# Attention and SwiGLU on one core: first scores and packing behind M, last output products inside the next batch's first chunk

## Chip, core and metric

The kernel runs on one core of one Trainium2 chip. The metric is device time in microseconds (us), as the median of several runs; less is better. The engines are called PE (TensorE: matmuls), DVE (VectorE), ACT (ScalarE), POOL (GpSimd) and SP (SyncE, which here only issues DMAs).

## What is computed

Two steps of attention, then a gated feed-forward layer, all in float32:

```python
batch, n_heads, seq, head_dim = (8, 8, 576, 64)
n_pack = 32
n_tokens, d_model, d_ff = (4608, 512, 1536)

def sm_attn(qq, kk, vv):
    s = scale * np.matmul(qq, kk.transpose(0, 1, 3, 2))
    s = s - np.max(s, axis=-1, keepdims=True)
    a = np.exp(s)
    a = a / (np.sum(a, axis=-1, keepdims=True) + 1e-09)
    return np.matmul(a, vv)
p_packed = sm_attn(p, k, v)              # 32 rows for each head
out = sm_attn(q, p_packed, p_packed)     # 576 rows for each head
...
g = x @ w_gate                           # x: out, heads side by side
silu = g * (1.0 / (1.0 + np.exp(-g)))
val = x @ w_val
return (silu * val @ w_out).astype(np.float32)
```

## The kernel before

**Tiles.** x itself is never formed. For each batch the kernel multiplies the packed rows by the gate and value weights; this product is called M, comes in six pieces k (`m_mm`, tile `w` by `ppt`, 64-row tiles of 32 columns), and is split into a high and a low part (`mh` on ACT, `ml` on DVE). The second attention's weights, also split (`a2h`, `a2l`), times M give gate and value directly. Every large product is made of three matmuls (high by low, low by high, high by high).

**Loops.** A batch b runs through 12 chunks fc of the inner width. A chunk has an A half (256 token columns) and a B half (320). Each half (`gv_chunk`) is a gate product and a value product of six matmuls each, into the two PSUM banks of the pool `ps_gv`: the gate bank is read by ACT (Silu into `sg`), the value bank by DVE (`hf`, and in B halves the 64 columns in `t`, kept in `t4`). ACT then makes `hh` from `hf` and DVE makes `hl`. With two banks in the pool, the next half's gate product waits for `sg`, and its value product for `hf` and `t`. Behind each half PE does six output matmuls (`out_mm` into `acc`) of the chunk before. In chunks of odd number M's next piece follows the A half.

**Filling.** While batch b runs, the attention of batch d = b + 1 is worked in between: scores of the first attention (`q_scores`, two groups of 32 matmul records), their maxima and differences on DVE (`q_read`), exponentials on ACT (`q_exp`), sums and a trip of the sums through DRAM (`q_sums`, `q_gather`: one DMA out, four back into `x`), common factors (`q_common`, `q_common_exp`, `q_factors`), scaling and transposing (`q_turn`), the packing product (`q_pack`, 160 records of 32 columns) and its transpose into `ppt`; then the second attention in two halves (`s2_mm`, `s2_block`, `s2_max`, `s2_exp`, `s2_sums` and `s2_scale`, `s2_turn`, `s2_high`, `s2_low`). `plan_of` says at which place of which chunk each step is issued. A place is a count of pieces of PE work in the chunk (1, 2: behind A's gate and value; 3, 4: behind the two output products; 5, 6 and 7, 8: the same for B) or "a", "ha" ("b", "hb"): behind the Silu of A (of B), and between `hh` and `hl`.

**Order.** PE runs in the order in which the code is written. DVE, ACT and SP are ordered by a scheduler, except that what goes through `pin` keeps the order of the program. Batch 0 has a hand-written order of its own (`PROGRAM`), ending in the output products of its last halves (`out22`, `out23`).

**End of a batch.** Behind chunk 11 come the last 12 output matmuls, then `end` copies the four `acc` banks out (`emit_out`). Behind each odd batch, the 64-column remainders of two batches, collected in `t4`, go through 36 more output matmuls into one bank `p4`:

```python
            outs(NFC - 1, 0, lambda: None)
            outs(NFC - 1, 1, lambda: None)
            end(rows, accs)
            if b % 2:
                p4 = ps()
```

Of the kernel before, what the change touches and what calls it, by code (L numbers as in the profile page):

```python
# [54 lines left out]
    out21 Ml:6.2 hl22 s2_low1 g23 s2_back0 silu23 out22 h23 hh23 s2_high0 hl23 s2_low0 out23  # L55
# [4 lines left out]
def tile_pack_attention_swiglu(ctx: ExitStack, tc: tile.TileContext, qT, kT, v, vq, pT, wgv, wout, out):  # L60
# [338 lines left out]
    def q_pack(b, half):  # L399

        if half == 0:
            sq[b].append(ps())
        a1, p_p = sq[b][4:]
        v_t = vs[b]
        for hp in range(2 * half, 2 * half + 2):
            for k in range(NKQ):
                for g in range(P // NP):
                    par, ds = g // 2, slice(g % 2 * NP, g % 2 * NP + NP)
                    nc.tensor.matmul(  # L409
                        p_p[NP * g : NP * g + NP, NP * hp : NP * hp + NP],  # L410
                        a1[:, par, hp, k, :], v_t[:, par, hp, k, ds],
                        start=(k == 0), stop=(k == NKQ - 1),
                    )
        if half:
            ppts[b] = pool.tile([P, P], F32, tag="ppt", bufs=2, name="ppt")
            pin(nc.vector.transpose(ppts[b], p_p[:, :P]))
            del sq[b], vs[b]
# [115 lines left out]
    def h_split(src, hi, lo, between=lambda: False):  # L533
        hh = pool.tile([P, 256], F32R, tag="hh", bufs=3, name="hh")
        hl = pool.tile([P, 256], F32R, tag="hl", bufs=3, name="hl")
# [54 lines left out]

    def plan_of(b):

        d, plan = b + 1, {}

        def at(fc, place, *todo):
            plan.setdefault((fc, place), []).extend(todo)

        if d < B:
            c, c2 = (1, 0) if d % 2 else (0, 1)
            cs, cs2 = slice(c, c + 1), slice(c2, c2 + 1)
# [4 lines left out]
            at(1, "ha", lambda: q_scores(d, 1, gv_ps), lambda: q_read(d, 1, (0, 1)))  # L608
            at(1, 8, lambda: q_sums(d, 0))
            at(2, "a", lambda: q_exp(d, 1))  # L610
            at(2, 8, lambda: q_sums(d, 1), lambda: q_gather(d))
            at(3, 8, lambda: q_common(d))
            if d + 1 < B:
                at(3, 8, lambda: load_k(d + 1))
            at(4, "a", lambda: q_common_exp(d))
            at(4, 4, lambda: q_factors(d))
            at(4, 8, lambda: q_turn(d, 0))
            at(5, 8, lambda: q_turn(d, 1))
            at(6, 4, lambda: q_pack(d, 0))
            at(6, 8, lambda: q_pack(d, 1))  # L620
            if d + 1 < B:
                at(7, "ha", lambda: load_v(d + 1))
            at(7, "ha", lambda: s2_tiles(d), lambda: s2_a2(d))
            at(7, "ha", lambda: s2_mm(d, c, gv_ps), lambda: s2_block(d, c))
# [4 lines left out]
            at(9, "ha", lambda: s2_mm(d, c2, gv_ps), lambda: s2_block(d, c2))  # L629
            if d + 1 < B:  # L630
                at(9, "ha", lambda: load_q(d + 1))
            at(9, 4, lambda: s2_low(d, c))
            at(9, 8, lambda: s2_max(d, cs2))
            at(10, "a", lambda: s2_exp(d, cs2))
            at(10, 4, lambda: s2_sums(d, cs2), lambda: s2_scale(d, cs2))
            at(10, 8, lambda: s2_turn(d, c2), lambda: s2_high(d, c2))
            at(11, 4, lambda: s2_low(d, c2))
        return lambda fc, place: bool([f() for f in plan.pop((fc, place), ())])

    with tc.manual_schedule(engines={mybir.EngineType.PE}):  # L640
# [6 lines left out]
        def begin(b):  # L647
            odd = b % 2
            if not odd:
                t4[b // 2] = pool.tile([P, NFC, P], F32, tag="t4", bufs=1, name="t4")  # L650
# [4 lines left out]
        def end(rows, accs):  # L655
            for i, r in enumerate(rows):
                emit_out(accs[i], r, i % 2)


        with tc.manual_schedule(  # L660
# [61 lines left out]
            rows, accs = begin(0)  # L722
# [121 lines left out]
        end(rows, accs)  # L844

        steady[0] = True
        for b in range(1, B):
            rows, accs = begin(b)
            run = plan_of(b)
            ha, hb = {}, {}  # L850

            def outs(fc, which, fill):
# [5 lines left out]
            for fc in range(NFC):  # L858
                count = [0]

                def fill():
# [10 lines left out]
                    if count[0] in (4, 8):  # L872
# [11 lines left out]
            end(rows, accs)  # L884
            if b % 2:
                p4 = ps()
                t4_t = t4.pop(b // 2)
                for fc in range(0, NFC, 2):
# [42 lines left out]
```

## Time and profile before

| | us |
|---|---|
| median of 3 runs (747.27 to 747.54) | 747.53 |
| span of the profiled execution, first to last instruction | 745.3 |
| what lies around the span (747.53 - 745.3) | 2.2 |
| PE busy | 732.5 (98%) |
| DVE busy | 456.8 (61%) |
| ACT busy | 368.8 (49%) |
| mean granted TensorE clock | 1.000 |

In rows of the timeline the first number is the start in us from the start of the span and the second is the time from the first start to the last end of the instructions merged in the row ("x2" are two). Ends of matmuls are modelled, and one begins long before the end of the one ahead of it. So this document reads PE's pace from starts: a row of x2 that begins at 237.10 and is followed by one at 237.34 took 0.24 us, whatever its own length says. In the groups the numbers behind the bar are busy us, mean ns of one, and idle us before them with what ended most of it.

### The profile page before, as it was taken

To read this page: it belongs to the slowest core of one execution; us is meant where nothing else is said; L and a number is where in the kernel's file an instruction comes from. 1 tells how busy PE (TensorE), PEld (TensorE's weight loads), DVE (VectorE), ACT (ScalarE), POOL (GpSimd) and SP (SyncE) were. 2 spreads that over 40 slices of the span, in tenths; PEclk is the share of its full clock that TensorE was granted. 3 is DMA by queue.
4 is the path that set the end of the run, shared out by engine and by line. 5 is a ranking of instruction groups with operands and counts; after the bars stand their busy time and mean duration, and the time that the engine had idled before them with its cause. 6 is when DMAs were issued, how large, how long until landed. Compare 5 with 4: busy or idle time off the path is not lost.

```text
span 745.3 us, 15149 instructions
## 1 busy us (share of the span) xinstructions
PE 732.5 (98%) x6288; PEld 594.8 (80%) x6288; DVE 456.8 (61%) x1008; ACT 368.8 (49%) x666; POOL 2.0 (0%) x13
## 2 busy tenths in 40 slices
PE   7999999999999999999999999999999999999998
PEld 5756666888788887887888888888888888888886
DVE  5988878665755557645765556655575555744334
ACT  3777755754516445563544535464452644533331
POOL 0000000000000000000000000000000000000000
PEclk9999999999999999999999999999999999999999
DMA  9696483201112021302112011100201000010001
GB/s 350 255 326 254 175 323 113 69 3 73 64 71 69 2 73 64 124 4 71 66 57 83 3 72 64 58 3 1 72 2 72 3 1 2 1 57 1 1 1 72
DMA packets 20005, 59.16 MB, mean 79 GB/s; under 512 B 5984, under 2 KB 7008, under 8 KB 17376
## 3 DMA queue, kind: packets, MB, share of 16 engines
q1 hardware_dynamic: 19792, 58.12, 21.6%
q8 instruction: 50, 0.82, 0.5%
q14 instruction: 19, 0.16, 0.1%
q10 hardware_dynamic: 144, 0.07, 0.0%
HBM read 48.69 MB, written 9.49 MB: 78 GB/s over the span
## 4 chain that ended last, share of the span: by engine, by line
PE 90%; DVE 5%; ACT 2%; issue 1%; DVEq 0%; ACTq 0%
PE gv L557 34%; PE acc L576 30%; PE aux L194 7%; PE gv L745 6%; PE acc L786 4%; PE aux L576 4%; PE aux L409 1%; PE gv_aux L194 1%; ACT L456 1%; PE acc L645 1%; DVE r L463 1%; DVE s L452 1%; DVE hf L568 1%; DVE hl L538 1%; DVE r L451 1%
## 5 line engine op out<-in xcount | busy, mean ns | idle before, releaser
L564 ACT ACTIVATE sg<-gv 128x256 f32<-128x256 f32 (+1 forms) x168 | 68.9, 410 | 165.3 <-PE gv L557 138.6
L557 PE MATMUL gv<-a2h,ml 128*128 128x256 f32 (+1 forms) x672 | 147.0, 300 | 1.8 <-DVE t L571 1.1
L568 DVE TENSOR_TENSOR hf<-gv,sg 128x256 f32<-128x256 f32 x168 | 70.8, 421 | 121.3 <-PE gv L557 99.3
L557 PE MATMUL gv<-a2l,mh 128*128 128x256 f32 (+1 forms) x672 | 144.0, 296 | 0.0
L557 PE MATMUL gv<-a2h,mh 128*128 128x256 f32 (+1 forms) x672 | 143.9, 295 | 0.0
L576 PE MATMUL acc<-wo_h,hl 128*128 128x512 f32 x344 | 140.7, 409 | 1.4 <-DVE hl L778 1.4
L576 PE MATMUL acc<-wo_l,hh 128*128 128x512 f32 x344 | 135.6, 394 | 0.0
L576 PE MATMUL acc<-wo_h,hh 128*128 128x512 f32 x344 | 134.5, 391 | 0.0
L557 PEld LDWEIGHTS gv<-a2h,ml 128*128 128x128 f32 x672 | 115.0, 189 | 18.4 <-PE gv L557 4.1
L105 ACT CAST hh<-hf 128x256 fp32r<-128x256 f32 x168 | 67.8, 403 | 102.8 <-DVE hf L568 102.8
L538 DVE TENSOR_TENSOR hl<-hf,hh 128x256 fp32r<-128x256 f32 x168 | 70.5, 420 | 78.3 <-ACT hh L105 78.3
L557 PEld LDWEIGHTS gv<-a2h,mh 128*128 128x128 f32 x672 | 108.4, 190 | 0.0
L557 PEld LDWEIGHTS gv<-a2l,mh 128*128 128x128 f32 x672 | 108.2, 189 | 0.0
L576 PEld LDWEIGHTS acc<-wo_h,hl 128*128 128x128 f32 x344 | 64.7, 188 | 37.0 <-issue 26.4
L576 PEld LDWEIGHTS acc<-wo_h,hh 128*128 128x128 f32 x344 | 64.6, 188 | 14.9
L576 PEld LDWEIGHTS acc<-wo_l,hh 128*128 128x128 f32 x344 | 64.8, 188 | 8.3 <-issue 0.5
L497 DVE TENSOR_TENSOR ml<-aux,mh 128x512 fp32r<-128x512 f32 x92 | 59.0, 683 | 4.7 <-ACT mh L523 3.6
L194 PE MATMUL aux<-w,ppt 64*32 64x512 f32 (+1 forms) x784 | 52.4, 588 | 0.5 <-ACT mh L523 0.5
L523 ACT CAST mh<-aux 128x512 fp32r<-128x512 f32 x92 | 49.2, 586 | 4.9 <-PE aux L194 1.9
L564 ACT ACT_TABLE_LOAD x30 | 38.5, 1283 | 16.4 <-PE gv L557 16.1
L786 PE MATMUL acc<-wo_f,h 128*128 128x512 f32 x80 | 37.2, 595 | 0.0
L786 PEld LDWEIGHTS acc<-wo_f,h 128*128 128x128 f32 x80 | 14.3, 189 | 13.8 <-issue 13.2
(152 smaller groups left out, 753.9 us busy)
## 6 DMA issues: line engine op xcount, KB each, us to landing
st<-in_wgv SPq DMA_DIRECT2D x12, 1024.0 KB, 6.3
k_t<-in_kT SPq DMA_DIRECT2D x16, 576.0 KB, 4.9
q_t<-in_qT SPq DMA_DIRECT2D x16, 576.0 KB, 4.9
out<-ot SPq DMA_DIRECT2D x36, 256.0 KB, 2.1
v_t<-in_vq SPq DMA_DIRECT2D x6, 1280.0 KB, 5.7
st<-in_wout SPq DMA_DIRECT2D x6, 1024.0 KB, 5.5
v_t<-in_v SPq DMA_DIRECT2D x2, 1024.0 KB, 8.7
p_t<-in_pT SPq DMA_DIRECT2D x7, 64.0 KB, 2.5
```

What stands on the lines that cost most here:

```text
L105: e.copy(dst, src)
L194: nc.tensor.matmul(outs[par][32 * hp : 32 * hp + 32], lhs(r, hp), rhs(r, hp), start=True, stop=True)
L409: nc.tensor.matmul(p_p[NP * g : NP * g + NP, NP * hp : NP * hp + NP], a1[:, par, hp, k, :], v_t[:, par, hp, k, ds], start=(k == 0), stop=( ...
L497: pin(nc.vector.tensor_tensor(*lows.pop(0), op=ALU.subtract))
L523: nc.scalar.copy(m[0][at], src)
L538: low = lo.tensor_tensor(hl, src, hh.bitcast(F32), op=ALU.subtract)
L557: nc.tensor.matmul(pg[:, :n], m_[:, g, f, s * P : (s + 1) * P], a_[:, g, off : off + n], start=(i == 0), stop=(i == 5),)
L564: nc.scalar.activation(sg[:, :n], pgs[0][:, :n], AF.Silu)
L568: nc.vector.tensor_tensor(hf, pgs[1][:, o : o + 256], sg[:, o : o + 256], op=ALU.mult)
L576: nc.tensor.matmul(acc[:, :], h_[:, c : c + P], w_[fc // 2][:, fc % 2], start=(fc == 0 and i == 0), stop=(fc == NFC - 1 and i == 2),)
L745: nc.tensor.matmul(held[i][s][:, :n], m_[:, g, f, s * P : (s + 1) * P], a_[:, g, off : off + n], start=(j == 0), stop=(j == len(todo) - 1),)
L786: nc.tensor.matmul(accs[2 * is_b + c], half(i)[:, c * P : c * P + P], wos[fc // 2][:, fc % 2], start=(fc == 0), stop=(fc == NFC - 1),)
```

## The change

Three things change.

1. The plan becomes two tables of places, one for d = 2 (`FIRST`) and one for all later batches (`LATER`). In `LATER` the first group of scores moves from chunk 0 of batch b to chunk 11 of the batch before it (chunk number -1), straight behind M's piece there, and into the gate and value banks (`gv_ps`) in place of the `aux` banks. In both tables the whole packing product is one step (`pack`) behind M's piece of chunk 5, also in a gate or value bank, in place of two halves at the ends of A and B in chunk 6. Many steps on DVE and ACT get other places: sums, common factors and turns come earlier, `max0` is issued in front of the B half of chunk 7, `sums0` between `hh` and `hl` of chunk 8's A half, `turn_0` and `turn_1` between `hh` and `hl` of a B half.
2. The output products of a batch's chunk 11 are no longer done at its end but behind the A and B half of the next batch's chunk 0 (`behind`). For batch 0 `out22` and `out23` go the same way. Behind an odd batch the 12 output matmuls stay where they were, and the 36 of `p4` go behind these two halves, 24 and 12. The bank `p4` and the splitting of `t4` have tiles of their own (`hh4`, `hl4`, two each).
3. `fill` now calls the plan at every count.

```diff
-        if d < B:
...
-            at(0, 2, lambda: q_scores(d, 0))
-            at(0, "ha", lambda: q_read(d, 0, (0,)))
-            at(0, "hb", lambda: q_read(d, 0, (1,)))
-            at(1, "a", lambda: q_exp(d, 0))
...
-            at(2, 8, lambda: q_sums(d, 1), lambda: q_gather(d))
-            at(3, 8, lambda: q_common(d))
-            at(4, "a", lambda: q_common_exp(d))
...
-            at(6, 4, lambda: q_pack(d, 0))
-            at(6, 8, lambda: q_pack(d, 1))
...
-            at(7, 8, lambda: s2_max(d, cs))
-            at(8, "a", lambda: s2_exp(d, cs))
-            at(8, 4, lambda: s2_sums(d, cs), lambda: s2_scale(d, cs))
-            at(8, 8, lambda: s2_turn(d, c), lambda: s2_high(d, c))
...
+LATER = """
+    -1.ha q0 q0r q0s
+    -1.b q0e
...
+    2.4 q1z
+    3.ha common
+    3.5 common_e
...
+    5.ha pack
...
+    8.ha sums0
...
+        "q0": lambda d: q_scores(d, 0, gv_ps if d > 2 else ps),
+        "pack": lambda d: q_pack(d, gv_ps),
+        for d in (b + 1, b + 2):
...
+            for line in (FIRST if d == 2 else LATER).strip().splitlines():
...
+                fc = int(fc) + NFC * (d - b - 1)
+                if (0 if d > 2 else -NFC) <= fc < NFC:
...
-    def q_pack(b, half):
+    def q_pack(b, bank=ps):
-        for hp in range(2 * half, 2 * half + 2):
+        for hp in range(NHP):
...
+        def last_outs(rows, accs, out):
+            def last(which):
+                out(which)
+                for c in range(2 * which, 2 * which + 2):
+                    emit_out(accs[c], rows[c], c % 2)
...
                 if fc:
                     outs(fc - 1, 0, fill)
+                else:
+                    behind(0)
...
                 if fc:
                     outs(fc - 1, 1, fill)
-            outs(NFC - 1, 0, lambda: None)
-            outs(NFC - 1, 1, lambda: None)
-            end(rows, accs)
+                else:
+                    behind(1)
+                    for x, y in zip((rows, accs), accs_of(b)):
+                        x.extend(y)
+            last = last_outs(rows, accs, lambda which: outs(NFC - 1, which))
+            if not b % 2:
+                return last
...
+            def behind_p4(which):
+                if which == 0:
+                    p4.append(ps())
+                    for k in range(4):
+                        mm4(k)
+                        split4(k + 2)
+                else:
+                    mm4(4, 5)
+                    emit_out(p4[0], (b // 2) * 2 * S + 4 * P, 0)
+
+            t4_t = t4.pop(b // 2)
+            split4(0, 1)
+            for which in range(2):
+                last(which)
+            return behind_p4
```

How rows move, at three places. The first is PE from M's piece in chunk 11 of batch 2 (`w_81` by `ppt`) to chunk 0 of batch 3; `acc` rows are output matmuls, `gv` rows gate and value products, `k_t,p_t` scores. Of each run the first row is shown. Before:

```order
L194 MATMUL aux<-w_81,ppt 32x512 x8
L576 MATMUL acc<-wo_h,hl 128x512
...
L557 MATMUL gv<-a2h,ml 128x320 x2
...
L576 MATMUL acc<-wo_h,hl 128x512
...
L557 MATMUL gv<-a2h,ml 128x256 x2
...
L323 MATMUL aux<-k_t,p_t 32x144 x16
L557 MATMUL gv<-a2h,ml 128x320 x2
```

And in the changed kernel:

```order
L257 MATMUL aux<-w_81,ppt 32x512 x8
L386 MATMUL gv_aux<-k_t,p_t 32x144 x16
L635 MATMUL acc<-wo_h,hl 128x512
...
L616 MATMUL gv<-a2h,ml 128x320 x2
...
L635 MATMUL acc<-wo_h,hl 128x512
...
L616 MATMUL gv<-a2h,ml 128x256 x2
...
L635 MATMUL acc<-wo_h,hl 128x512
...
L616 MATMUL gv<-a2h,ml 128x320 x2
```

The scores moved from between chunk 0's halves to behind M, and where 18 output matmuls stood in one run there are now six behind each of three halves.

The second place is PE in chunks 5 and 6 of batch 2, where the packing product (`v_t` by `a`) of batch 3 stands. Before:

```order
L194 MATMUL aux<-w_84,ppt 32x512 x8
L576 MATMUL acc<-wo_h,hl 128x512
...
L409 MATMUL aux<-v_t,a_2705 32x32 x40
L557 MATMUL gv<-a2h,ml 128x320 x2
...
L409 MATMUL aux<-v_t,a_2705 32x32 x40
L557 MATMUL gv<-a2h,ml 128x256 x2
```

And in the changed kernel:

```order
L257 MATMUL aux<-w_84,ppt 32x512 x8
L470 MATMUL gv_aux<-v_t,a_2659 32x32 x80
L635 MATMUL acc<-wo_h,hl 128x512
```

Two halves, each between output and gate matmuls, became one step between M and the output matmuls.

The third place is DVE in chunk 8 of batch 2, from `hf` of the A half to `t` of the B half; `r` and `s` belong to the second attention's sums. Before:

```order
L568 TENSOR_TENSOR hf<-gv,sg 128x256
L538 TENSOR_TENSOR hl<-hf,hh 128x256
L463 TENSOR_REDUCE r_2961<-s_2960 128x18
L464 TENSOR_SCALAR r_2961<-r_2961 128x18
L465 RECIPROCAL r_2961<-r_2961 128x18
L469 TENSOR_TENSOR s_2960<-s_2960,r_2961 128x576
L568 TENSOR_TENSOR hf<-gv,sg 128x256
L571 TENSOR_TENSOR t_2322<-gv,sg 128x64
```

And in the changed kernel:

```order
L627 TENSOR_TENSOR hf<-gv,sg 128x256
L523 TENSOR_REDUCE r_2921<-s_2920 128x18
L524 TENSOR_SCALAR r_2921<-r_2921 128x18
L525 RECIPROCAL r_2921<-r_2921 128x18
L529 TENSOR_TENSOR s_2920<-s_2920,r_2921 128x576
L597 TENSOR_TENSOR hl<-hf,hh 128x256
L627 TENSOR_TENSOR hf<-gv,sg 128x256
L630 TENSOR_TENSOR t_2292<-gv,sg 128x64
```

The sums now stand in front of `hl`, so they no longer wait for `hh`.

More of the change, by code (lines that the diff above doesn't have):

```diff
@@ L54 @@
     s2_exp0 wout_low11 s2_exp1 hl21 s2_sums1 g22 M:6.2 s2_back1 silu22 out18 Mh:6.2 h22 hh22 s2_sums0 s2_high1
-    out21 Ml:6.2 hl22 s2_low1 g23 s2_back0 silu23 out22 h23 hh23 s2_high0 hl23 s2_low0 out23
+    out21 Ml:6.2 hl22 s2_low1 g23 s2_back0 silu23 h23 hh23 s2_high0 hl23 s2_low0
+"""
+FIRST = """
+    0.2 q0
+    0.b q0r
+    0.hb q0s
+    1.2 q0e
+    1.ha q1 q1r
+    2.a q1e
+    2.7 q0z
+    2.8 q1z
+    3.2 common
+    3.a common_e factors
+    4.5 load_k
+    4.b turn0
+    4.hb turn1
+    5.ha pack
+    6.b load_v
+    6.7 tiles
+    7.ha mm0 block0
+    7.3 max0
+    8.a exp0 sums0
+    8.7 turn_0
+    9.ha mm1 block1
+    9.3 high0 low0
+    9.hb max1 exp1
+    9.7 load_q
+    9.8 sums1
+    10.hb turn_1
+    11.3 high1
+    11.hb low1
+"""
+LATER = """
+    -1.ha q0 q0r q0s
+    -1.b q0e
+    1.ha q1 q1r
+    1.4 q0z
+    2.a q1e
+    2.4 q1z
+    3.ha common
+    3.5 common_e
+    3.hb factors
+    4.a turn0
+    4.4 load_k
+    4.5 turn1
+    5.ha pack
+    6.7 tiles
+    7.ha mm0 block0
+    7.3 max0
+    7.7 load_v
+    8.a exp0
+    8.ha sums0
+    8.hb turn_0
+    9.a high0
+    9.ha mm1 block1
+    9.b low0
+    9.hb max1 exp1
+    9.7 load_q
+    10.1 sums1
+    10.hb turn_1
+    10.8 high1
+    11.4 low1
 """
@@ L397, in q_turn @@
         ))
[L399 to L405 removed]
+    def q_pack(b, bank=ps):
+        p_p = bank()
+        a1, v_t = sq[b][4], vs[b]
+        for hp in range(NHP):
             for k in range(NKQ):
```

122 lines of the change are left out of this document (69 added, 53 removed).

## The prediction

> **What bounds the kernel.** I read the page first.
>
> ```profile
> PE 732.5 (98%) x6288; PEld 594.8 (80%) x6288; DVE 456.8 (61%) x1008; ACT 368.8 (49%) x666; POOL 2.0 (0%) x13
> ```
>
> PE is busy for 98% of the span; no other engine comes near. That does not mean that nothing can be won: ends of matmuls are modelled, so a gap of 0.2 us between two of them does not show as idle. The next view is therefore the timeline of PE, read by starts. Regular paces are there: two gate or value matmuls of 256 columns in 0.24 us, two of 320 in 0.29, one output matmul in 0.23. What exceeds them is what can be removed. I went through batch 2 and its end and then looked for the same places in the others. Nothing but three kinds of excess came up: a change from one tile form to another, a wait for a gate or value bank, and the wait at the end of batch 0.
>
> **Changes of form, as they stand before.** First M alone (chunk 3), then scores alone (chunk 0), then chunk 1, where M and scores already stand together:
>
> ```profile
> 238.06 0.40 PE L557 MATMUL gv<-a2h,mh 128*128 128x256 f32 x2
> 238.39 1.09 PE L194 MATMUL aux<-w,ppt 64*32 64x512 f32 x16
> 239.41 0.50 PE L576 MATMUL acc<-wo_h,hl 128*128 128x512 f32 x1
> ...
> 220.36 0.72 PE L323 MATMUL aux<-k_t,p_t 64*32 64x144 f32 x32
> 221.01 0.56 PE L557 MATMUL gv<-a2h,ml 128*128 128x320 f32 x2
> ...
> 223.34 0.40 PE L557 MATMUL gv<-a2h,mh 128*128 128x256 f32 x2
> 223.84 0.47 PE L557 MATMUL gv<-a2h,ml 128*128 128x256 f32 x2
> 224.15 0.40 PE L557 MATMUL gv<-a2l,mh 128*128 128x256 f32 x2
> ...
> 224.71 1.09 PE L194 MATMUL aux<-w,ppt 64*32 64x512 f32 x16
> 225.59 0.75 PE L323 MATMUL gv_aux<-k_t,p_t 64*32 64x144 f32 x32
> 226.27 0.50 PE L576 MATMUL acc<-wo_h,hl 128*128 128x512 f32 x1
> 226.61 0.40 PE L576 MATMUL acc<-wo_l,hh 128*128 128x512 f32 x1
> ```
>
> Going into the narrow form costs 0.09 us (238.06 to 238.39 is 0.33, not 0.24), coming back 0.11 (226.27 to 226.61 is 0.34, not 0.23). M alone holds PE 1.02 us, but 0.88 when scores follow it: the last 0.14 is its running out, which scores of the same form cover.
>
> **Scores behind M.** Alone they cost 0.09 + 0.65 + 0.11 = 0.85 us. Behind M they cost 0.68 - 0.14 = 0.54, since M pays the way in and out. That is 0.3 us for each batch with the later table whose scores move, d = 3 to 7: 5 x 0.3 = **1.5 us**. They now need the gate and value banks of the A half of chunk 11; chunk 1's scores, above, already do, at the same distance from the same work, and the gate product after them starts on time.
>
> **The whole packing product behind M.** Before, in chunk 6:
>
> ```profile
> 259.79 0.39 PE L576 MATMUL acc<-wo_h,hh 128*128 128x512 f32 x1
> 260.10 0.90 PE L409 MATMUL aux<-v_t,a 128*32 128x32 f32 x80
> 260.93 0.56 PE L557 MATMUL gv<-a2h,ml 128*128 128x320 f32 x2
> 261.33 0.45 PE L557 MATMUL gv<-a2l,mh 128*128 128x320 f32 x2
> ```
>
> Each half costs 0.08 in, 0.83, and 0.11 out: 1.02, so 2.04 for both. No row shows a packing product behind M, whose tiles have 64 rows and not 128. Bounds: if this is a change of form like any other, M keeps its 1.02 and the pack adds 0.08 + 1.66, which saves 0.3; if it follows M as scores do, the pack adds 1.66 - 0.14, which saves 0.52, and about 0.1 more (an estimate) if joining the halves spares one running out. I take 0.45, in the middle, since the way out is certainly paid once less: 6 x 0.45 = **2.7 us**, with 1.8 and 3.7 as ends.
>
> [...]
>
> **Waits for a bank at a batch's start.** In the same rows the value product of chunk 1 starts at 223.84: 0.50 instead of 0.24 after the row ahead, and its first pair takes 0.31. That is 0.33 us in which PE waits for `hf` and `t` of chunk 0's B half, because chunk 0 has no output products behind B that would cover them. With the last six outputs of the batch before in that place (1.4 us) the wait goes; I find it in all seven batches. The moved outputs are not free: in a run they are a little faster than six at a time.
>
> ```profile
> 206.57 0.39 PE L576 MATMUL acc<-wo_h,hl 128*128 128x512 f32 x1
> ...
> 210.68 0.39 PE L576 MATMUL aux<-wo_h,hl 128*128 128x512 f32 x1
> ```
>
> Eighteen in a run take 4.11, against 18 x 0.231 = 4.17. So six boundaries (1 to 2, up to 6 to 7) give 6 x (0.33 - 0.06) = **1.6 us**.
>
> **The end of batch 0.** Here a wait is traded for a smaller one.
>
> ```profile
> 123.36 0.39 PE L576 MATMUL acc<-wo_h,hh 128*128 128x512 f32 x1
> 125.12 0.50 PE L576 MATMUL acc<-wo_h,hl 128*128 128x512 f32 x1 [1.37 <-DVE hl L778]
> ...
> 123.93 0.20 DVE L770 TENSOR_TENSOR t<-gv,sg 128x64 f32<-128x64 f32 x1
> ```
>
> PE waits 1.76 - 0.23 = 1.53 for the last `hl`, and 0.11 for the new start. In the changed kernel chunk 0's A half of batch 1 starts at 122.20 instead. Its gate product is free, but its value product, due at 122.92, needs the bank that `t` leaves at 124.13; with 0.15 for the handing over it starts at 124.28: a new wait of 1.36 and 0.07. By then `hl` is done. With chunk 1's 0.33, 1.53 + 0.11 + 0.33 - 1.43 = **0.5 us**.
>
> **The wait in chunk 9.** Batch 2, with the DVE and ACT work that it hangs on:
>
> ```profile
> 279.31 0.40 PE L557 MATMUL gv<-a2h,mh 128*128 128x256 f32 x2
> 279.93 0.47 PE L557 MATMUL gv<-a2h,ml 128*128 128x256 f32 x2 [0.22 <-DVE t L571]
> ...
> 276.92 0.43 DVE L538 TENSOR_TENSOR hl<-hf,hh 128x256 fp32r<-128x256 f32 x1 [1.92 <-ACT hh L105]
> 277.27 0.75 DVE L463 TENSOR_REDUCE r<-s 128x18 f32<-128x576 f32 x1
> ...
> 279.23 0.42 DVE L568 TENSOR_TENSOR hf<-gv,sg 128x256 f32<-128x256 f32 x1
> 279.57 0.21 DVE L571 TENSOR_TENSOR t<-gv,sg 128x64 f32<-128x64 f32 x1
> ...
> 275.91 0.69 ACT L456 ACTIVATE s<-s 128x576 f32<-128x576 f32 x1
> ...
> PE gv L557 <- DVE t L571: 1.1, 5, 0.2
> ```
>
> PE loses 0.62 - 0.24 = 0.38 and, as in chunk 1, 0.07 for the late start: 0.45. It is so in batches 1 to 6 (0.31 once, else 0.44 to 0.45 by starts); the last row, of the view of waits, has five of them, each shortened by the modelled ends. DVE is late: `hl` waits for `hh`, which ACT makes behind the exponential; then come the sums (277.27 to 279.2, 2.0 us), and only then `hf` and `t`. In the new order the sums follow the exponential directly, at 276.6, and end at 278.6; `hl` 0.35, `hf` 0.34, `t` 0.21: the bank is free at 279.5 and not 279.78. PE wants it at 279.55, less 0.15 for the handing over, so 0.1 would remain; but `max0` now stands ahead of B's `hf` in chunk 7 and not behind `hl`, so the exponential itself, which here began its table load only behind `max0`, starts about 0.4 earlier. So I take the whole wait as gone: 2.6 us over six batches, and with the 0.07 of a late start that the turn of the second half causes in chunk 11, **3.0 us**. Without the earlier exponential it would be about 2; if the order brings nothing, 0.
>
> **What is now close.** Two new chains end just where PE needs a bank. The first: the exponential of the moved scores now stands in front of chunk 0's A half, with the reload of the Silu table between. Chunk 2 shows such a reload in front of a B half:
>
> ```profile
> 233.73 0.45 PE L557 MATMUL gv<-a2h,ml 128*128 128x320 f32 x2
> ...
> 234.85 1.28 ACT L564 ACT_TABLE_LOAD   x1 [0.30 <-PE gv L557]
> 236.14 0.44 ACT L564 ACTIVATE sg<-gv 128x320 f32<-128x320 f32 x1
> ```
>
> From the start of the gate product to the end of `sg` are 2.85 us; for an A half 0.16 less (gate product) and 0.06 less (Silu), 2.63. PE comes back for the bank after 1.43 + 1.39 = 2.82. It holds, by 0.19 less 0.15.
>
> The second: the common factors move into chunk 3.
>
> ```profile
> 234.58 0.43 DVE L538 TENSOR_TENSOR hl<-hf,hh 128x256 fp32r<-128x256 f32 x1 [1.54 <-ACT hh L105]
> ...
> 237.85 0.75 DVE L350 TENSOR_REDUCE z<-e 128x4 f32<-128x576 f32 x1
> ...
> 238.63 0.33 SPq L356 DMA_DIRECT2D zd<-z  x1
> 240.04 1.75 SPq L358 DMA_DIRECT2D x<-zd  x4
> ...
> x<-zd SPq DMA_DIRECT2D x24, 8.0 KB, 1.7
> ...
> 239.57 1.07 ACT L523 CAST mh<-aux 128x512 fp32r<-128x512 f32 x2
> ...
> 244.05 0.40 PE L557 MATMUL gv<-a2h,ml 128*128 128x256 f32 x2
> ```
>
> The sums before the trip now stand right behind `hl` of chunk 2's A half (the first row, done at 235.0), 2.85 earlier than 237.85, so the first DMA goes at 235.8 and the last `x` lands at 235.8 + 1.4 + 1.3 + 1.7 = 240.2 (the wait for the first DMA, the issue of four, the landing). DVE reaches the factors at about 239 and stands until then, with `hl` and both `ml` behind it; they end at about 242.3, and PE wants `ml` at 244.05. ACT loads the table for the exponential when `mh` is done (240.64), needs the factors at 241.92, reloads, and ends `sg` of the B half at 242.1 + 1.28 + 0.44 = 243.8; PE comes for that bank at 244.05. It holds by 0.1. For these two places, for batch 1's chunk 5 (a turn now ahead of `hf`) and for `hl` of chunk 11 at odd ends I put down -0.4 us (nothing to -2).
>
> DMAs move too (the loads of k and v by a chunk or less), but are needed a batch later. The last batch's tail keeps its order: no change.
>
> **The sum.** 1.5 + 2.7 + 1.6 + 0.5 + 3.0 - 0.4 = 8.9 us. The span of 745.3 becomes 736.4. Around the span lie 2.2 us up to the median of the runs, 747.5, so that the time is 747.5 - 8.9 = **738.6 us**.
>
> **Rivals.**
> - *New waits replace the old* (15%): chunk 9's bank stays late, since `hf` still stands behind the same 2 us of DVE work, and the two close places each lose 0.2 us in five batches. The sum loses 3.0 and 2.0: 743.6. For it: margins of 0.1. Against it: the rows give positive margins everywhere.
> [...]
> - *Slower, by the trip through DRAM* (4%): DVE and, behind it, ACT stand for `x` in chunk 3. From a landing 1.2 us later than worked out (241.4) each further us is a us of PE in front of chunk 4, in five batches. To eat 8.9 us and 1.5 more, `x` must land 1.2 + 2.1 = 3.3 us late, 7.7 after the first DMA's issue and not 4.4; at 4 late the time is 747.5 - 8.9 + 5 x 2.8 = 752.6. The rows speak against it: 24 landings have a median of 1.7 and SP has nothing else to send then.
> - *It does not do what it says* (4%): PE's work is the same, and what looks like waits and changes of form is pace that comes back elsewhere. Then 747.
> - *More than forecast* (8%): pack follows M like scores, and no margin fails: 736.8.
>
> The forecast has 65%. 8 times in 10 the time lies from 736.5 to 743.5: below stands the sum with its best ends (1.5 + 3.7 + 1.6 + 0.5 + 3.0 = 10.3, 737.2, less a little), above most of the first rival. A difference under 0.2% (1.5 us) is about what measurement can't tell from none. Faster by more: 0.91; within: 0.04; slower: 0.05.
>
> **What would show it.** In the changed kernel's timeline: scores and pack rows directly behind M, M's 16 matmuls holding 0.88 with scores behind it, and 0.88 (or 1.02) with the pack; no 0.5 in chunk 1's rows and no 0.62 in chunk 9's; at the end of batch 0 a wait of about 1.4 in chunk 0's A half; chunk 0's B half and chunk 4's A half starting without a gap. A gap at one of the last two, or DVE standing for `x` past the time at which the factors are needed in chunk 3, would make the prediction wrong.

## The result, and the profile after

The changed kernel took 744.1 us (median of 4 runs, 742.52 to 744.29) against 747.53 (median of 4, 747.27 to 748.81): a ratio of 0.9948, with 0.9934 to 0.9962 as 95% interval. So it is faster by 3.4 us. The prediction of 738.6 us promised 8.9, and its range ended at 743.5. The profiled execution took 742.52 us with a span of 740.7, that is 4.6 us less span than before and not 8.9.

The page says little, as before: TensorE is busy all the time.

```profile
span 740.7 us, 15176 instructions
PE 726.7 (98%) x6288; PEld 595.3 (80%) x6288; DVE 448.8 (61%) x1008; ACT 372.1 (50%) x666; POOL 2.0 (0%) x13
...
q8 instruction: 50, 0.82, 0.5%
```

The timeline of PE is read by starts, as in the prediction. First the end of batch 0, then the end of batch 1 (shared tile `p4`) with chunk 1 of batch 2, the pack in that batch, and its chunk 9:

```profile
122.63 0.40 PE L616 MATMUL gv<-a2h,mh 128*128 128x256 f32 x2
124.23 0.47 PE L616 MATMUL gv<-a2h,ml 128*128 128x256 f32 x2 [1.20 <-DVE t L826]
...
212.28 0.39 PE L635 MATMUL aux<-wo_h,hl 128*128 128x512 f32 x1
...
217.86 0.46 PE L616 MATMUL gv<-a2h,ml 128*128 128x320 f32 x2
...
219.62 0.39 PE L635 MATMUL aux<-wo_h,hl 128*128 128x512 f32 x1
...
222.42 0.40 PE L616 MATMUL gv<-a2h,ml 128*128 128x256 f32 x2
...
222.90 0.40 PE L616 MATMUL gv<-a2h,mh 128*128 128x256 f32 x2
223.14 0.40 PE L616 MATMUL gv<-a2h,ml 128*128 128x256 f32 x2
...
250.83 1.09 PE L257 MATMUL aux<-w,ppt 64*32 64x512 f32 x16
251.85 1.56 PE L470 MATMUL gv_aux<-v_t,a 128*32 128x32 f32 x160
253.34 0.50 PE L635 MATMUL acc<-wo_h,hl 128*128 128x512 f32 x1
253.68 0.39 PE L635 MATMUL acc<-wo_l,hh 128*128 128x512 f32 x1
...
278.05 0.40 PE L616 MATMUL gv<-a2h,mh 128*128 128x256 f32 x2
278.29 0.40 PE L616 MATMUL gv<-a2h,ml 128*128 128x256 f32 x2
```

Most of what was forecast is there. The wait of 1.36 at the end of batch 0 is there (124.23 - 122.63 - 0.24). Chunk 1's value product starts 0.24 behind the row ahead (223.14), not 0.50. In chunk 9, too, the value product starts 0.24 behind the row ahead (278.29), not 0.62. The pack starts 1.02 behind M's start and takes 1.49 (253.34 - 251.85); with the way out of 0.11, which M would otherwise have paid, it adds 1.50 and not 2.04: 0.54 less, more than the 0.45 forecast. M kept its 1.02 in front of it, as in the first of the prediction's two bounds; what was saved was each half's way in and out (0.08 and 0.11), and some 0.17 by joining them (1.49 and not twice 0.83).

But the first and the sixth pack look otherwise, in the same view:

```profile
158.73 1.09 PE L257 MATMUL aux<-w,ppt 64*32 64x512 f32 x16
159.75 1.35 PE L470 MATMUL gv_aux<-v_t,a 128*32 128x32 f32 x135
162.21 0.40 PE L470 MATMUL gv_aux<-v_t,a 128*32 128x32 f32 x25 [1.11 <-issue]
...
598.84 1.40 PE L470 MATMUL gv_aux<-v_t,a 128*32 128x32 f32 x141
601.53 0.38 PE L470 MATMUL gv_aux<-v_t,a 128*32 128x32 f32 x19 [1.29 <-issue]
```

After 135 and 141 of 160 records PE stops. From start to start of the records around them the stops are 1.31 and 1.49 us. "Issue" means that nothing in the profile released it: no semaphore came. No pack of the kernel before does this.

The other loss is in the tail, on VectorE:

```profile
725.41 0.69 DVE L170 COPY ot<-acc 128x512 f32<-128x512 f32 x1 [0.67 <-PE acc L635]
729.76 0.69 DVE L170 COPY ot<-acc 128x512 f32<-128x512 f32 x1 [3.66 <-DMA out<-ot]
730.37 0.28 DVE L170 CAST hh<-t 128x256 fp32r<-128x256 f32 x1
730.69 0.43 DVE L597 TENSOR_TENSOR hl<-t,hh 128x256 fp32r<-128x256 f32 x1
```

The eviction of the third accumulator stands until one of the two output buffers has been written out, and the third pair of the last shared tile (730.37) is queued behind it. PE waits 1.12 for that pair (a gap of 1.35 between products that follow each other in 0.23), and the 36 products take 9.76 us to the modelled end of the last, where the kernel before took 8.32.

### The profile page after: what moved, and what is told of

Same layout as the page of the kernel before. It is cut to its first block, busy times and chain, and to the rows that moved or that the text cites. A ratio compares the mean times of both kernels' runs of the same rounds, so it can differ in the third digit from the quotient of the medians.

```text
span 740.7 us, 15176 instructions
## 1 busy us (share of the span) xinstructions
PE 726.7 (98%) x6288; PEld 595.3 (80%) x6288; DVE 448.8 (61%) x1008; ACT 372.1 (50%) x666; POOL 2.0 (0%) x13
## 4 chain that ended last, share of the span: by engine, by line
PE 95%; DVE 2%; issue 1%; DMA 0%; ACT 0%; DVEq 0%; ACTq 0%
PE gv L616 36%; PE acc L635 33%; PE aux L257 7%; PE gv L801 6%; PE acc L842 4%; PE aux L635 4%; PE gv_aux L470 1%; PE gv_aux L257 1%; PE gv_aux L386 1%; PE acc L704 1%; DMA out<-ot 0%; DVE ot L170 0%; ACT mh L583 0%; PE aux L333 0%; DVE s L529 0%
## 5 line engine op out<-in xcount | busy, mean ns | idle before, releaser
L616 PE MATMUL gv<-a2h,ml 128*128 128x256 f32 (+1 forms) x672 | 143.9, 296 | 1.2 <-DVE t L826 1.2
L616 PEld LDWEIGHTS gv<-a2h,ml 128*128 128x128 f32 x672 | 116.8, 189 | 16.3 <-issue 1.4
```

The lines of the kernel that those rows point to most:

```text
L616: nc.tensor.matmul(pg[:, :n], m_[:, g, f, s * P : (s + 1) * P], a_[:, g, off : off + n], start=(i == 0), stop=(i == 5),)
```

## The experiments

The theories are: A, PE's instructions come in blocks of 256 (the changed kernel's profile has 50 packets of the instruction queue and 12,775 rows of PE), and a pack eats a block faster than the next one comes; B, the pack waits for data or for memory. "Stop" means a gap inside the pack, from start to start. Times are medians; the kernel before, run beside them, took 747.5 to 747.8 us.

| run | us (lowest to highest) | ratio to before, 95% interval |
|---|---|---|
| shift52 | 742.2 (741.67 to 744.39) | 0.9935, 0.9913 to 0.9956 |
| shift128 | 743.61 (743.27 to 744.54) | 0.9946, 0.9931 to 0.9961 |
| halves | 741.91 (741.8 to 742.25) | 0.9922, 0.9907 to 0.9937 |
| tail | 742.29 (742.07 to 742.54) | 0.9926, 0.9912 to 0.9941 |
| sand_tail | 742.83 (742.57 to 743.56) | 0.9935, 0.9923 to 0.9948 |
| again | 743.32 (742.75 to 744.57) | 0.9942, 0.9929 to 0.9954 |
| ends | 748.34 (747.59 to 749.01) | 1.0005, 0.9996 to 1.0013 |
| chunk9 | 745.07 (744.6 to 746.04) | 0.9963, 0.995 to 0.9977 |
| split_tail | 741.36 (740.52 to 743.14) | 0.9923, 0.9909 to 0.9937 |
| scores0 | 751.67 (751.2 to 752.95) | 1.0053, 1.0041 to 1.0066 |
| ends_scores | 746.48 (745.81 to 747.19) | 0.9982, 0.9973 to 0.9991 |
| stream | 763.02 (one run) | |

**shift52 and shift128: the same work, at other places in the stream.** Both add tiny products behind a warm-up, far ahead of the packs (below shift52; shift128 has `warm_up(4)` and `tiny(34)`).

```diff
+        def tiny(n, at=warm_ps):
+            for _ in range(n):
+                nc.tensor.matmul(at[:32, :32], ident[:, :32], ident[:, :32], start=True, stop=True)
...
             warm_up(6)
+            tiny(13)
```

> The changed kernel with 52 more TensorE instructions (13 tiny products of 32x32) behind the second warm-up, so that every later instruction stands 52 places further on. In the changed kernel the six packs (starts 159.8, 251.9, 334.4, 425.6, 508.0, 598.8 us) hold 160 records each; the first and the sixth stop for 1.31 and 1.49 us after 135 and 141 records. Theory A (instruction supply): TensorE's instructions come in blocks of 256, a block is ordered when the one before it is entered and takes some 2.5 us, and a pack of 320 instructions that runs through a whole block in 1.2 us runs dry. The packs then begin at places 38, 166, 224, 96, 154 and 26 of a block (242, 114, 172, 44, 102, 230 before): the stops of the first and the sixth pack go, the third gets one of 1.3 to 1.5 us, and the second at most 0.2. Span 740.7 - 1.31 - 1.49 - 0.19 + 1.4 = 739.1 us, with up to 0.3 more for the added products. Theory B (the pack waits for data, v or the turned exponentials, or shares the memory with a load): nothing in the data flow is touched, so the first and the sixth pack stop as before and the others do not; span 740.7 to 741.0.

> The same with a shift of half a block: 136 instructions added (34 tiny products) and 8 taken away (two warm-up products), 128 in sum. Theory A: the packs begin at places 114, 242, 44, 172, 230, 102 of a block, so the stops move from the first and the sixth pack to the second and the fifth (1.3 to 1.5 us each), about 0.2 behind the fourth, none in the first, third and sixth; span 740.7 plus or minus 0.4. Theory B: stops in the first and the sixth pack as before, span 740.7.

Of shift52, in the timeline of PE, the packs that stopped for longer than 0.2 us:

```profile
160.04 1.13 PE L470 MATMUL gv_aux<-v_t,a 128*32 128x32 f32 x109
161.69 0.65 PE L470 MATMUL gv_aux<-v_t,a 128*32 128x32 f32 x51 [0.52 <-issue]
...
334.43 1.43 PE L470 MATMUL gv_aux<-v_t,a 128*32 128x32 f32 x144
336.90 0.33 PE L470 MATMUL gv_aux<-v_t,a 128*32 128x32 f32 x16 [1.05 <-issue]
```

And of shift128:

```profile
252.05 1.35 PE L470 MATMUL gv_aux<-v_t,a 128*32 128x32 f32 x135
254.72 0.40 PE L470 MATMUL gv_aux<-v_t,a 128*32 128x32 f32 x25 [1.33 <-issue]
...
336.04 1.11 PE L470 MATMUL gv_aux<-v_t,a 128*32 128x32 f32 x106
339.01 0.67 PE L470 MATMUL gv_aux<-v_t,a 128*32 128x32 f32 x54 [1.85 <-issue]
...
511.39 1.40 PE L470 MATMUL gv_aux<-v_t,a 128*32 128x32 f32 x141
513.97 0.38 PE L470 MATMUL gv_aux<-v_t,a 128*32 128x32 f32 x19 [1.19 <-issue]
```

The stops moved as A said: in shift52 the sixth pack's is gone but for 0.11 and the third has one (1.24); in shift128 the second and the fifth have them (1.53, 1.39), after 135 and 141 records, and the first and sixth none. B falls: data and loads were the same. Two stops were not expected: 0.71 in shift52's first pack and 2.05 in shift128's third. Both are at the first end of a block within the pack, after 109 and 106 records, so there the next block took longer (3.1 and 4.8 us) than the 2.5 us assumed. The spans, 739.9 instead of 739.1 and 742.7 instead of 740.7, hold other differences too: in both runs the tail is 1.2 us shorter than in the changed kernel's profile.

The place says more than the time. If all of PE's rows are counted in order (matmuls, weight loads and the semaphore rows between them), all 18 stops of more than 0.1 us without a releaser inside a pack, in seven profiles (the changed kernel, again, shift52, shift128, tail, sand_tail and stream), stand behind the same row of 256.

**halves: the pack part alone undone.**

```diff
-    5.ha pack
+    6.4 pack0
+    6.8 pack1
-        p_p = bank()
+        if half == 0:
+            sq[b].append(ps())
-        for hp in range(NHP):
+        for hp in range(2 * half, 2 * half + 2):
```

> The changed kernel with the pack alone undone: two halves of 80 records behind the outputs of chunk 6, in the auxiliary banks, as in the kernel before; all else as changed. Theory A: 160 instructions in a row never run through a block of 256, so no pack stops anywhere; each of the six packs gives back the 0.54 us that the second, fourth and fifth pack gained: 740.7 - 2.99 + 6 x 0.54 = 740.9 us of span, that is: merging the pack was worth nothing. Theory B (the stop belongs to the data of these two batches): 2.8 us of waits stay in the first and sixth pack, span 743.7.

No stop in any of the twelve halves, and the span was 740.2, not the 743.7 of B. In the median it is 741.91, below every one of the nine runs of the changed kernel (742.52 to 744.57, median 743.65 with those of again). So merging the pack was not worth 2.7 us. That it cost the 1.7 us between these medians is not shown: in halves the copy in the tail stood 2.22 us, in both profiles of the changed kernel 3.66 and 3.9, and from the last M to the end are 32.6 us, there 33.8 and 34.0. The run tail has the merged pack and a tail of 32.6, and took 0.4 us more than halves.

**again: is the spread the clock or the stops?** The changed kernel, untouched.

> The changed kernel once more, untouched. Its four first times spread over 1.8 us (742.5 to 744.3) while the version with halves spread over 0.45 us with granted clocks from 0.997 to 1.000. Theory A: the stops depend on how long each block of instructions takes to come, so the times spread by 1.5 us or more again, and this profile shows stops of other lengths than the first one (1.31, 0, 0.19, 0, 0, 1.49 us). Rival (the clock): the spans go with the granted clock alone, and the stops are those of the first profile within 0.2.

The times spread by 1.8 us again. This profile (span 742.8) has stops of 1.87, 0, 0, 0.08, 0 and 1.52 us, 0.7 more than the first, and loses 0.47 behind the third pack, where the first loses 0.19. So the length varies from execution to execution while the place stays, as A has it. The clock does not tell the two apart by itself: here it was 0.997 to 0.999, in halves it was 0.997 to 1.000 with spans from 740.0 to 740.4. What share of the spread is the clock stays open.

**tail: buffers of their own for two evictions.**

```diff
-        ot = pool.tile([P, DM], F32, tag="ot", bufs=2, name="ot")
+        ot = pool.tile([P, DM], F32, tag="ot", bufs=2, name="ot") if own is None else io_tile(own, [P, DM], F32, "ot")
...
+            if b == B - 1:
+                steady[0] = "tail"
```

> The changed kernel with buffers of their own for the evictions of the third and fourth accumulator of the last batch (the other two keep the two output buffers). Theory C: in the last batch VectorE's eviction of the third accumulator stands 3.66 us for an output buffer to be written out, the pairs of the last shared tile stand behind it, and the 36 products of that tile take 9.76 us where the kernel before took 8.32; with buffers of their own the copy runs at once, the 36 take 8.3 us, and the span falls by 1.4 to 739.3 us. Rival: the pairs are late because only two of them are held at a time (a third needs the products of the first to be done) and not for the copy: the 36 stay at 9.5 or more, span 740.4 or more.

The second copy now runs as soon as its products end, and the 36 products take 8.53 us and not 9.76:

```profile
726.25 0.69 DVE L170 COPY ot<-acc 128x512 f32<-128x512 f32 x1 [0.67 <-PE acc L635]
727.61 0.69 DVE L170 COPY ot<-acc 128x512 f32<-128x512 f32 x1 [0.67 <-PE acc L635]
729.69 0.29 DVE L170 CAST hh<-t 128x256 fp32r<-128x256 f32 x1 [1.39 <-PE aux L635]
```

The mechanism is shown; the rival falls, as the pairs still wait for PE's products and the 36 run through. The span fell by 0.4 only, since this execution lost 0.8 us more in and behind its packs than the first profile, and the time by 1.0 to 1.8, according to which runs of the changed kernel it is compared with. One thing takes size from it: without these buffers the copy stood 3.66 and 3.9 us in both profiles of the changed kernel, but only 2.2 to 2.5 in the other seven profiles with this tail, whose 36 products took 8.53 to 8.56.

The traces show what goes with it. In the changed kernel (both profiles), tail, sand_tail and split_tail a packet of the instruction queue begins 0.6 us behind the issue of the first of these outputs, which lands after 3.3 to 3.8 us; in the other seven none begins within 3 us, and it lands after 2.1 to 2.3. So late landing, too, goes with the place in the stream of instructions in these twelve profiles, and the short tail of shift52, shift128 and halves was luck.

**sand_tail: M between the two halves.**

```diff
-        "pack": lambda d: q_pack(d, gv_ps),
+        "pack": lambda d: (q_pack(d, 0), m_part(d - 1, 3, both), q_pack(d, 1)),
```

> The changed kernel with the pack cut in two around M: 80 records, the M of chunk 5 (16 row groups, 1.02 us), 80 records, all directly one behind the other; and with the last batch's two evictions in buffers of their own, as in the run before. Theory A (instruction supply): a block of 256 instructions now holds M whenever it runs through the pack, and takes at least 0.5 + 1.0 + 0.5 + 0.2 = 2.3 us, about as long as the supply (2.3 to 2.7 us in the runs so far); the stops shrink to 0.4 or less each. Against the version with halves in chunk 6 (741.9) each pack keeps most of the 0.54 us of a place behind M and pays one more change of form (0.1 to 0.2): 741.9 - 6 x 0.35 = 739.8 us, between 739.0 and 741.0. Theory B: stops as in the changed kernel, 743 or more. If the changes of form around M cost as much as the place saved: 742.

The forecast failed. The stops stayed, with M inside the block:

```profile
598.71 0.90 PE L472 MATMUL gv_aux<-v_t,a 128*32 128x32 f32 x80
599.54 1.09 PE L257 MATMUL aux<-w,ppt 64*32 64x512 f32 x16
600.56 0.73 PE L472 MATMUL gv_aux<-v_t,a 128*32 128x32 f32 x61
602.83 0.38 PE L472 MATMUL gv_aux<-v_t,a 128*32 128x32 f32 x19 [1.54 <-issue]
```

The two ends of blocks lie 256 instructions apart, at 598.95 (after the 29th record) and 602.83: 3.88 us, not 2.3 to 2.7. The trace's packets of the instruction queue say why. In the changed kernel's profile each takes 0.88 to 1.65 us, but around the packs it mostly begins either within 0.2 us or 0.8 to 1.1 us behind the start of the block before (here 599.95, 1.00 behind); it was 0.45 in shift52's first pack and 1.9 in shift128's third. Where a stop ended a block, the block had lasted between 2.1 us (shift52's sixth pack) and 4.8 (shift128's third).

**split_tail: half behind M, half where it was.** Each half has a bank and a transposition of its own.

```diff
-    5.ha pack
+    5.ha pack0
+    6.4 pack1
...
+        at = slice(64 * half, 64 * half + 64)
-        pin(nc.vector.transpose(ppts[b], p_p[:, :P]))
+        pin(nc.vector.transpose(ppts[b][:, at], p_p[:, at]))
```

> The changed kernel with the pack in two halves in banks of their own, each half turned by itself: 80 records directly behind the M of chunk 5 as in the change, 80 behind the first outputs of chunk 6 as in the kernel before; and the last batch's two evictions in buffers of their own. Theory A, as corrected by the run with M between the halves (a block of instructions takes 2.4 to 4.1 us from its order to its first use): 160 instructions in a row leave at least 96 slower ones in any block, 5 us or more, so nothing stops. Against the version with both halves in chunk 6 (741.9) the first half gains half of the 0.54 us in each of six batches: 741.9 - 1.6 = 740.3 us, between 739.6 and 741.2. If the stops have another cause they stay in the first and the sixth batch's half behind M: 742 or more.

No stop in the twelve halves; the half of the sixth pack behind M, where the changed kernel stopped, runs through:

```profile
598.22 1.09 PE L259 MATMUL aux<-w,ppt 64*32 64x512 f32 x16
599.24 0.90 PE L472 MATMUL gv_aux<-v_t,a 128*32 128x32 f32 x80
```

By starts of M, each batch gains 0.20 to 0.22 us on halves, 1.25 in six (forecast 1.6). The span is 738.7 and the median 741.36, the lowest of all, though 0.2 above the range expected; its runs overlap with those of halves, so that it is the better of the two is not shown. Both beat the changed kernel's median.

**stream: the price by itself.**

```diff
             warm_up(6)
+            tiny(300)
```

> The disputed cost by itself: the changed kernel with 300 tiny products of 32x32 (600 records, 1200 instructions) behind the second warm-up, where nothing but the constant identity is read. Theory A: they run dry after each 256 instructions; a block takes 2.4 to 4.1 us in place of 1.2, the whole 11 to 18 us. Later instructions stand 1200 places further on (176 in a block), so the packs begin at 162, 34, 92, 220, 22, 150: a stop in the fourth pack, none in the first and sixth. Theory B: 600 records at 9.3 ns, 5.6 us, without a stop, and the stops of the first and the sixth pack stay.

Half of it held. In the timeline the 300 products take 23.0 us (8.71 to 31.74), but they stop only once:

```profile
8.71 5.35 PE L708 MATMUL warm_ps<-ident 128*32 128x32 f32 x163
16.40 15.41 PE L708 MATMUL warm_ps<-ident 128*32 128x32 f32 x437 [2.34 <-issue]
```

At most 32 of their records start in a us: 31 ns each and not the pack's 9.3. They all write one quarter of a bank's rows, where the pack's products take the four quarters in turn; whether that slows them was not tried. A block so lasts 4 us or more by itself, and mostly its successor is there in time. The kernel could therefore not show a train of stops. What it did show is the third shift: a stop in the fourth pack, as A said, none in the first and sixth, and 0.37 in the fifth.

```profile
446.26 1.45 PE L470 MATMUL gv_aux<-v_t,a 128*32 128x32 f32 x146
449.02 0.33 PE L470 MATMUL gv_aux<-v_t,a 128*32 128x32 f32 x14 [1.32 <-issue]
```

**chunk9: the new places of DVE's score block alone, in the kernel before.**

```diff
-            at(8, 4, lambda: s2_sums(d, cs), lambda: s2_scale(d, cs))
-            at(8, 8, lambda: s2_turn(d, c), lambda: s2_high(d, c))
+            at(8, "ha", lambda: s2_sums(d, cs), lambda: s2_scale(d, cs))
+            at(8, "hb", lambda: s2_turn(d, c))
+            at(9, "a", lambda: s2_high(d, c))
...
-            at(9, 4, lambda: s2_low(d, c))
-            at(9, 8, lambda: s2_max(d, cs2))
+            at(9, "b", lambda: s2_low(d, c))
+            at(9, "hb", lambda: s2_max(d, cs2), lambda: s2_exp(d, cs2))
...
```

> The kernel before with one part of the change alone: in later batches the sums, the turn and the high half of the first score block, and the maximum, exponential and sums of the second, stand at the places of the new table (half a chunk earlier), nothing else is moved. The prediction: the wait of 0.45 us ahead of chunk 9's products in six batches and the 0.07 us in chunk 11 go, 3.0 us: 747.5 - 3.0 = 744.5 us. Rival: the wait is only pushed on, to chunk 10 or 11 or to the Silu of the next chunk: 747.0 to 747.5 us.

The time fell by 2.75 us against the 747.82 of the kernel before, run beside it. In chunk 9:

```profile
279.61 0.40 PE L557 MATMUL gv<-a2h,mh 128*128 128x256 f32 x2
279.92 0.47 PE L557 MATMUL gv<-a2h,ml 128*128 128x256 f32 x2
```

0.31 where 0.62 was. By starts of M each batch gains 0.29 to 0.31 in chunk 9 and 0.05 to 0.09 behind it, 2.2 us in six; 0.15 a batch stays. This run leaves `max0` where it was, behind B's `hl` in chunk 7, so the exponential is not earlier: the case in which the prediction said that 0.1 would remain, and the term be about 2. In halves, where `max0` is earlier too, the whole 0.45 goes. The rival (the wait pushed on) falls.

**ends, scores0, ends_scores: the other two parts, undone in halves.** ends does a batch's last outputs at its own end; scores0 moves the first scores out of chunk 11 into chunk 0; ends_scores does both, with the scores where the kernel before had them. First the core of ends, then that of scores0.

```diff
             if not b % 2:
-                return last
+                last(0)
+                last(1)
+                return done
...
-    -1.ha q0 q0r q0s
-    -1.b q0e
+    0.ha q0 q0r q0s
+    0.b q0e
```

> The version with halves (741.9 us), with the batches' ends undone as well: each batch's last output products and evictions stand at its own end again, the shared tile's pairs and products behind them. The prediction gave this part 1.6 us for six boundaries and 0.5 for the end of batch 0: 741.9 + 2.1 = 744.0 us. Read from the steps of the traces it is 0.55 for batch 0, 0.27 for each of three even batches and 0 to 0.1 for the odd ones, whose 36 products of the shared tile hid the wait before: 741.9 + 1.4 = 743.3 us. If the ends are worth nothing: 741.9.

> The version with halves in chunk 6 (741.9 us) with the first score products of the next batch but one moved back from behind the M of chunk 11 into chunk 0, behind the first two groups of gv products (five batches). The prediction gave this part 5 x 0.3 = 1.5 us: 743.4. Rival: the exponential moves with the scores, and its table load now collides with other waits of chunk 0 or 1, as one was seen to do in the run with the ends undone: 744 or more. If the place behind M is worth nothing: 741.9.

> The version with halves, with the batches' ends and the first scores both undone, at the places of the kernel before. The run with the ends alone undone gave 748.3 us where the prediction's terms said 744.0; its trace has 1.24 us of waiting ahead of chunk 0's second group after even batches, behind an exponential and a Silu table load at the batch's end. If that is the scores' early exponential laid bare by the missing outputs (the two parts need each other), undoing both gives the prediction's terms: 741.9 + 1.5 + 2.1 = 745.5, or with the ends as read from the steps 744.8. If the ends alone are worth 6.4 us: 748.3 + 1.5 = 749.8.

Either part alone undone costs far more than its term: 6.4 us for the ends, 9.8 for the scores. Both undone cost 4.6; in the profiles 0.9 of it lies ahead of the first later M (116.35 in halves, 117.23 here), where nothing was changed, and the 3.7 behind it answer to the 3.6 of the prediction's terms. The parts need each other. In ends, after batch 2:

```profile
304.28 0.40 PE L621 MATMUL gv<-a2h,mh 128*128 128x256 f32 x2
305.77 0.56 PE L621 MATMUL gv<-a2h,ml 128*128 128x320 f32 x2 [1.08 <-ACT sg L628]
...
304.04 1.28 ACT L628 ACT_TABLE_LOAD   x1 [1.55 <-PE gv L621]
```

PE waits 1.25 for the bank of a Silu whose table has to be loaded again (304.04), since the early scores' exponential stands in front of it. The moved outputs are its cover: the prediction's margin of 0.04 in front of chunk 0's A half held because they stand there. In scores0 the exponential, its table load and the reload stand in chunk 0, and each of five batches loses 1.23 to 1.26 us up to chunk 1's M and 0.70 up to chunk 3's; which of its waits makes the second loss was not followed.

## Why the prediction was wrong

Without the pack the sum was 6.2 us; halves measured 5.6 in the median. The comparison by starts of M, halves against before, shows every part but the pack, in one profile each:

| step of the prediction | forecast | measured in halves |
|---|---|---|
| scores behind M and boundaries (1.5 + 1.6) | 3.1 | 2.69: 0.57, 0.57 and (without scores) 0.34 after even batches, 0.40 to 0.41 three times after odd ones |
| end of batch 0 | 0.5 | 0.53 |
| chunks 9 and 11 | 3.0 | 3.07: 0.50 to 0.53 in each of six |
| close places | -0.4 | -0.7: 0.06 four times, 0.41 once |
| tail | 0 | -0.2 (in the changed kernel's two profiles -1.5 and -1.7) |

- **The pack failed.** The term "6 x 0.45 = 2.7 us" was right for what a change of form costs (0.54 was saved where nothing stopped), and overlooked that 160 products of 9.3 ns in one piece consume instructions faster than they come (256 of them in 1.19 us, where a block took 2.1 or more). Halves of 80, 3 us apart, never did. With stops of 1.31, 0.19 (behind the third pack) and 1.49 us the first profile gained 3.24 - 2.99 = 0.25. Against halves the merged pack loses 0.4 us in the medians where the tail is the same (tail), which the two intervals do not tell from none. So it brought nothing or a little less, and that is about 3 of the 5.5 us by which the time was missed. The upper end of the term's bounds was sought among changes of form; its lower end should have gone below nothing.
- **"The last batch's tail keeps its order: no change" was wrong.** PE's order is kept, DVE's is not: two copies now stand ahead of pairs three to six. When the outputs land late, as in both profiles of the changed kernel, this tail takes 1.5 and 1.7 us more than before, when early 0.2. Those 0.2 are not the copies: they stay in tail, where the copies run at once. The 36 products follow each other at 0.232 us there and not at 0.227; why was not tried.
- **The end of batch 0, the waits in chunks 1 and 9, the scores behind M**: right, mechanism and size. Only the boundaries after odd batches gave 0.17 less each. There the 36 products of the shared tile, 8.16 in one run before (210.68 to 218.84), now take 5.58 and 2.80 in two pieces; that adds up to 0.22. It is the same slower pace and not the cut: in ends_scores they stand in one piece and follow each other at 0.232 us. (In the prediction's term for the boundaries 18 x 0.231 is 4.16 and not 4.17, which changes nothing.)
- **The close places** held, and the trip through DRAM is the narrow one. The view of waits for DVE, before and in the changed kernel:

```profile
DVE y L367 <- DMA x<-zd: 0.6, 1, 0.6
```

```profile
DVE y L430 <- DMA x<-zd: 7.9, 5, 2.5
```

DVE now stands in five batches, as forecast. Only when `x` is late does PE feel it: in halves a stand of 2.79 us goes with the 0.41 of the table, and in shift52, where DVE stood 3.25 us once, PE lost 0.78 in front of chunk 4. So the rival "slower, by the trip" exists, at about a tenth of its price. The instruction queue is in this, too: in the twelve profiles with the new tables, the 39 stands of at most 1.61 us had no packet of it beginning in the 5.5 us before their end, and the 21 of 1.97 us or more had one each.
- **The reload of the Silu table** in front of chunk 0's A half took what it took in chunk 2 before (1.29, from 234.85 to 236.14): Silu starts 1.30 us behind its load's start (301.18 and 299.88 in the changed kernel).

Of the 5.5 us missed, the pack so has about 3, the tail 1.5, the boundaries 0.4 and the close places 0.3. What is left of the 1.6 us between the changed kernel's profiled execution (742.52) and its median (744.1) is not settled: stops, landings and the clock all vary.

## What to carry to other kernels

Before merging small matmuls into one uninterrupted run, count their instructions and compare the time of a block of them (here 256, 1.19 us) with the time in which a block arrives, read from the instruction queue's packets in one's own trace (here 2.1 to 4.8 us); here runs of 160 never stopped, and two of the changed kernel's six runs of 320 did, for 1.31 and 1.49 us. When such a run stops with "issue" as its releaser, shift the stream by a known number of instructions: here the stops moved with shifts of 52 and 128, which spoke for supply; had they stayed, that would have spoken for data. A shift moves the landing of small transfers as well (the first of the last outputs landed after 2.1 to 2.3 us in seven profiles, shift52's and shift128's among them, after 3.5 in the changed kernel's), so a gain between two kernels can be one of place. A part whose cover is another part cannot be priced by undoing it alone (here 6.4 and 9.8 us for one of two, 4.6 for both).

## What the runs showed of the hardware

PE's instructions came in packets of 16.4 KB (0.82 MB in 50), one for some 256 of its 12,775 rows (12,576 of matmuls and weight loads, 199 of semaphores and drains). In the changed kernel the two stops end 8192 = 32 x 256 of these rows apart. A block took 2.1 to 4.8 us from the start of its predecessor to its first use where PE ran out, while the pack eats 256 instructions in 256 / 320 x 1.49 = 1.19 us. Such a packet also goes with late transfers: in the fourteen profiles the 42 output transfers behind whose issue a packet began 0.2 to 1.3 us later landed after 2.9 to 4.3 us, while of the 408 with none near (from 0.9 us ahead of the issue to 2.0 behind) 390 landed within 2.6 and half within 2.05. How a packet holds them up is not shown. Ahead of the changed kernel's first stop a packet begins at 159.88, 0.07 behind the start of a block, and the next block is entered at 162.21; ahead of the sixth pack's stop one begins at 598.91, 0.04 before the start of a block, and the next is entered at 601.53. Why the blocks came no sooner is not shown.
